# Attention totals summed behind the next product, and a 66-column spread of the maxima

## The chip, the cores and the metric

The kernel runs on one core of one Trainium2 chip. The metric is device microseconds of one execution; the runs of a kernel are given with their median.

## The reference

Two blocks run one after the other. The first is attention with hashed buckets over q, k and v of shape 4 x 8 x 768 x 64; the second is a gated MLP over the attention's output.

```python
mask = q_bucket[:, :, :, None] == k_bucket[:, :, None, :]   # 6 sign bits of q @ proj, k @ proj
scores = np.where(mask, (q @ k.T) / 8, -1e9)
attn = np.exp(scores - max(scores));  attn = attn / (attn.sum(-1) + 1e-9)
x = attn @ v                                     # heads side by side: 4 x 768 x 512
h = gelu(x @ w_in);  u, v = h[..., :512], h[..., 512:]
v_s = w_sg @ layer_norm(v) * g_ln + b_sg         # along the sequence
out = x + (u * v_s) @ w_out
```

## The kernel before, in words

**Attention.** Two heads make a pair (16 pairs), and the 768 queries of a pair are worked on in two halves of 384: 32 half pairs. `prepare` loads a pair (q, k, v), transposes q and k on TensorE (L500), splits them into a high and a low part, and computes the bucket features (L520). For each half pair:

- `largest` computes the masked scores of 128 queries against all keys (L540) and VectorE takes the maximum of each row into `mx` (L545), three times for a half pair.
- `shift` takes the minimum of the two negated maxima into column 0 and column 64 of `m` (L552, VectorE), transposes `m` by a product with the identity (L558: three matmuls, 128 weight columns each), and ScalarE copies the rows 0 and 64 of the result into the feature rows of q (L564), so that the maximum is subtracted within the next product.
- `weigh` computes the scores of 128 keys against 384 queries (L578, three products that split float32 into parts, and the features), and ScalarE takes the exponential into `p` (L582), six times. GpSimd adds the six up into `sum` (L595).
- `weighted` is the product of `p` with v (L606): 24 matmuls, in which the two heads stand in two column groups of 64 columns. `p` has a 385th column of ones, so that column 384 of the result is the sum of v over the keys.
- `finish` sums `sum` over the partitions with a product with ones (`total`, L621: eight matmuls in four column groups of 32 columns), adds 1e-9 (L624), takes the sums through DRAM to spread them (L629, L630), takes the reciprocal (L631), brings it back through DRAM to all partitions (L633, L635), and multiplies (L641). Three ScalarE instructions (L638 to L640) and a GpSimd addition (L642) put the mean of v in the place of rows that have no partner. L643 writes the half to DRAM.

A step handles two key tiles of `weigh` and, four steps ahead (`AHEAD`), one call of `largest`; a half pair has three steps.

**The MLP.** For each batch: `hidden_v` (L774), `hidden_u` (L805), `gate` (L823), `project` (L849, and the residual by transposes, L854). `weight_job` splits the float64 weights into two float32 parts on VectorE and GpSimd (L368 to L385); `gate_weights` transposes w_sg (L733).

**What sets the order.** Every piece is handed to a planner (`Plan.add`) with an engine, a cost, a priority and what it reads and writes; `Plan.order` simulates the engines and writes the order of each engine's queue out by hand. The constants at the top (`MLP`, `HID`, `AVP`, `S0P`, `PREP`, `SHIFTP`, `FINP`, `WSTEP`, `WP`) are offsets of those priorities; the lower number comes first among pieces that can start. TensorE's results go to eight PSUM banks of one tile `psb`; a score takes two banks side by side, the product, the total and the spread one each. The DMAs of the attention are issued by SyncE.

```python
plan.add(PE, 1.3 * HT, prio, product, p + [st.v], [av], form="col")          # weighted, L608
plan.add(PE, 0.375, prio, total, [sums], [tp], form="col32")                  # finish, L623
weighted(sts[n], 2 * g + AVP)                                                 # L681
finish(sts[n], hf, 2 * g + FINP)                                              # L682
```

## Time and profile before

| | |
|---|---|
| median of 3 runs | 790.71 us (790.6 to 790.88) |
| span of the profiled execution | 791.5 us |
| PE busy | 767.8 us (97%) |
| DVE, ACT, POOL busy | 536.9, 421.1, 481.0 us |
| mean granted TensorE clock | 0.993 |

The span is the time from the first to the last instruction of the one execution that was profiled; nothing of that execution's time lies outside it in the profile. It is 0.8 us over the median of the runs. PE is TensorE's matmuls, PEld its weight loads, DVE is VectorE, ACT is ScalarE, POOL is GpSimd, SP is SyncE. Matmuls overlap, so that the end of a matmul in a row lies after the start of the next; the pace is read from the starts.

### The profile page before, as it was taken

To read this page: it belongs to the slowest core of one execution; us is meant where nothing else is said; L and a number is where in the kernel's file an instruction comes from. 1 tells how busy PE (TensorE), PEld (TensorE's weight loads), DVE (VectorE), ACT (ScalarE), POOL (GpSimd) and SP (SyncE) were. 2 spreads that over 40 slices of the span, in tenths; PEclk is the share of its full clock that TensorE was granted. 3 is DMA by queue.
4 is the path that set the end of the run, shared out by engine and by line. 5 is a ranking of instruction groups with operands and counts; after the bars stand their busy time and mean duration, and the time that the engine had idled before them with its cause. 6 is when DMAs were issued, how large, how long until landed. Compare 5 with 4: busy or idle time off the path is not lost.

```text
span 791.5 us, 14719 instructions
## 1 busy us (share of the span) xinstructions
PE 767.8 (97%) x5480; PEld 613.0 (77%) x5480; DVE 536.9 (68%) x862; ACT 421.1 (53%) x742; POOL 481.0 (61%) x522
## 2 busy tenths in 40 slices
PE   4999999999999999999999999799999999999998
PEld 3777776767677676767767669798898889988996
DVE  7978888989889888666766437868932167407630
ACT  2366576666656665655655566625632266116511
POOL 1478889898878778776867774665742235404230
PEclk9899999999999999999999999999999999999999
DMA  7032443245334414321320123400115311040003
GB/s 204 23 77 69 110 116 99 70 112 124 74 97 94 104 47 91 92 70 53 82 58 25 32 54 138 144 28 28 43 64 160 100 60 41 1 150 12 1 0 133
DMA packets 99304, 60.91 MB, mean 77 GB/s; under 512 B 64288, under 2 KB 91040, under 8 KB 99232
## 3 DMA queue, kind: packets, MB, share of 16 engines
q1 hardware_dynamic: 97920, 56.94, 26.5%
q10 hardware_dynamic: 1312, 3.02, 1.2%
q8 instruction: 43, 0.70, 0.4%
q14 instruction: 29, 0.24, 0.1%
HBM read 47.16 MB, written 12.78 MB: 76 GB/s over the span
## 4 chain that ended last, share of the span: by engine, by line
PE 86%; DVE 8%; DMA 2%; ACT 1%; issue 1%; POOL 0%; DVEq 0%; ACTq 0%; POOLq 0%; SPq 0%
PE psb L578 16%; PE psb L606 16%; PE psb L823 13%; PE psb L540 10%; PE psb L849 8%; PE psb L774 6%; PE psb L805 5%; PE psb L520 5%; PE psb L500 2%; DVE mx L545 2%; PE psb L621 2%; PE psb L558 2%; PE psb L854 1%; DVE m L552 1%; DMA sq<-s 1%
## 5 line engine op out<-in xcount | busy, mean ns | idle before, releaser
L595 POOL TENSOR_TENSOR sum<-sum,p 128x384 f32<-128x384 f32 x256 | 243.6, 983 | 8.4 <-ACT p L582 8.4
L545 DVE TENSOR_REDUCE mx<-psb 128x2 f32<-128x768 f32 x192 | 174.7, 952 | 63.1 <-PE psb L540 61.8
L582 ACT ACTIVATE p<-psb 128x768 f32<-128x768 f32 x192 | 145.7, 812 | 61.6 <-PE psb L578 60.2
L606 PE MATMUL psb<-p,v 128*64 128x385 f32 x768 | 131.2, 491 | 0.0
L606 PEld LDWEIGHTS psb<-p,v 128*64 128x64 f32 x768 | 52.3, 137 | 64.0 <-issue 62.8
L595 POOL TENSOR_TENSOR sum<-p,p 128x384 f32<-128x384 f32 x64 | 64.2, 1026 | 60.9 <-ACT p L582 60.9
L540 PE MATMUL psb<-fk,fq 64*128 64x384 f32 x384 | 72.6, 372 | 2.8 <-DVE mx L545 1.7
L759 DVE SCALAR_TENSOR_TENSOR h<-h,psb 128x384 f32<-128x384 f32 (+1 forms) x56 | 32.8, 606 | 58.5 <-ACT h L758 58.5
L834 POOL TENSOR_TENSOR gs<-gt,gs 128x384 fp32r<-128x384 f32 x32 | 33.2, 1041 | 59.2 <-ACT gs L831 59.2
L578 PE MATMUL psb<-hq,hk 64*128 64x384 f32 x384 | 68.8, 352 | 0.0
L540 PE MATMUL psb<-hk,hq 64*128 64x384 f32 x384 | 65.5, 335 | 0.0
L849 PE MATMUL psb<-woh,gs 128*128 128x512 f32 x192 | 65.4, 402 | 0.0
L578 PE MATMUL psb<-fq,fk 64*128 64x384 f32 x384 | 65.1, 332 | 0.0
L578 PE MATMUL psb<-lq,hk 64*128 64x384 f32 x384 | 65.0, 332 | 0.0
L578 PE MATMUL psb<-hq,lk 64*128 64x384 f32 x384 | 64.9, 332 | 0.0
L823 PE MATMUL psb<-wgh,zh 128*128 128x384 f32 x192 | 64.3, 335 | 0.0
L823 PE MATMUL psb<-wgh,zl 128*128 128x384 f32 x192 | 64.2, 334 | 0.0
L823 PE MATMUL psb<-wgl,zh 128*128 128x384 f32 x192 | 64.2, 334 | 0.0
L540 PEld LDWEIGHTS psb<-fk,fq 64*128 64x128 f32 x384 | 36.6, 185 | 30.2 <-issue 13.0
L826 DVE TENSOR_TENSOR gt<-psb,b_bc 128x384 f32<-128x384 f32 x32 | 17.8, 556 | 58.4 <-PE psb L823 34.9
L784 POOL TENSOR_TENSOR mv<-mv,epsr 128x1 f32<-128x1 f32 x24 | 14.1, 588 | 67.8 <-DVE mv L783 67.7
L626 ACT COPY un<-psb 128x385 f32<-128x385 f32 x32 | 15.5, 483 | 68.2 <-PE psb L606 68.2
(127 smaller groups left out, 1751.8 us busy)
## 6 DMA issues: line engine op xcount, KB each, us to landing
q<-in_q_dram SPq DMA_DIRECT2D x32, 192.0 KB
k<-in_k_dram SPq DMA_DIRECT2D x32, 192.0 KB
v<-in_v_dram SPq DMA_DIRECT2D x16, 384.0 KB
rs<-r SPq DMA_DIRECT2D x64, 96.0 KB
xs<-xt SPq DMA_DIRECT2D x32, 192.0 KB
x<-xs SPq DMA_DIRECT2D x16, 384.0 KB
rx<-xs SPq DMA_DIRECT2D x96, 64.0 KB
out_dram<-ob SPq DMA_DIRECT2D x24, 256.0 KB
```

What stands on the lines that cost most here:

```text
L520: nc.tensor.matmul(fp()[:, hf, :SH], w[:, s, :], x()[:, hf * SH:(hf + 1) * SH], start=(i == 0), stop=(i == 2))
L540: nc.tensor.matmul(sc[kh]()[:, j, :SH], x[0]()[row(j), qs], x[1]()[row(j), kh * SH:(kh + 1) * SH], start=(n == 0), stop=(n == 1))
L545: plan.add(DVE, 0.95, prio, lambda kh=kh: nc.vector.tensor_reduce(mx()[:, kh, i, :], sc[kh]()[:, :, :SH], axis=AX.X, op=ALU.max, negate=Tr ...
L578: nc.tensor.matmul(sc[i]()[:, j, :SH], x()[row(j), ks], y()[row(j), cs], start=(n == 0), stop=(n == 3))
L582: plan.add(ACT, 0.81, prio, lambda i=i: nc.scalar.activation(p[i]()[:, :, :SH], sc[i]()[:, :, :SH], AF.Exp), [sc[i]], [p[i]])
L595: plan.add(POOL, 1.03, prio + 0.6, lambda i=i, j=j, first=first: nc.gpsimd.tensor_add(sums()[:, j], (first or sums)()[:, j, :SH], p[i]()[: ...
L606: nc.tensor.matmul(av()[row(j), :SH + 1], st.v()[:, j, kt, :], p[kt]()[:, j, :], start=(kt == 0), stop=(kt == NT - 1))
L774: nc.tensor.matmul(ps(), x()[:, ts_], w[:, c, FH:FF], start=(c == 0 and n == 0), stop=(c == NC - 1 and n == 2))
L805: nc.tensor.matmul(ps()[:, :SH], w[:, c, fs], x()[:, cs], start=(c == 0 and n == 0), stop=(c == NC - 1 and n == 2))
L823: nc.tensor.matmul(vp()[:, :SH], z()[:, t, fs], w()[:, t, cs], start=(t == 0 and n == 0), stop=(t == NT - 1 and n == 2))
L834: nc.gpsimd if e == POOL else nc.vector).tensor_sub(gl()[:, cs], gt(), gh()[:, cs].bitcast(F32)),
L849: nc.tensor.matmul(po(), a()[:, ts_], w()[:, f, :], start=(f == 0 and n == 0), stop=False)
```

## The change

1. `total` is no piece of its own any more. `weighted` of a half pair is given the half pair before it (`owed`) and runs the eight matmuls of its total right behind its own product, in one piece. `finish` of a half pair therefore comes one half pair later; `last` runs the one total that is left at the end. `sum` gets three buffers, `un` four.
2. The three ScalarE instructions and the GpSimd addition for rows without a partner go. The 385th column of `p` holds 1e-9 / 768 in the place of 1, and one VectorE instruction computes (un + column 384) x reciprocal.
3. `mx` has a third column that holds the constant `EMPTY`, and the minimum is a `tensor_reduce` over it in the place of a `scalar_tensor_tensor` with two operands from SBUF. The spread loads 66 columns of `m` as weights in the place of 128.
4. The priority constants change, among them those of the weight splitting (`WSTEP`, `WP`) and of the MLP's weights (`MLP`), and the planner's cost for a piece with two forms.

```diff
-MLP = {"xl": "POOL", "gm": "DVE", "gl": "POOL", "wg": 463.45, "wo": -43.61, "x": 464.83}
+MLP = {"xl": "POOL", "gm": "DVE", "gl": "POOL", "wg": 450.21, "wo": 213.95, "x": 464.55}
+NSUM = 3
-HID = 277.32
-AVP = 3.21
-S0P = 0.22
+HID = 276.04
+AVP = 2.54
+S0P = 2.0
-PREP, SHIFTP, FINP, WSTEP, WP = 4.15, -4.68, 2.34, 48.11, -68.38
+PREP, SHIFTP, FINP, WSTEP, WP = 3.93, -3.05, 8.67, 59.98, 9.42
...
-            (nc.vector if i % 2 else nc.gpsimd).memset(t[:, :, SH:SH + 1], 1.0)
+            (nc.vector if i % 2 else nc.gpsimd).memset(t[:, :, SH:SH + 1], 1e-9 / S)
...
-            plan.add(DVE, 0.16, prio, lambda: V.scalar_tensor_tensor(
-                m()[:, :, MROW::BL], mx()[:, 0], EMPTY, mx()[:, 1], op0=ALU.min, op1=ALU.min),
-                     [mx], [m], port=True)
+            W = BL + 2
+            plan.add(DVE, 0.16, prio, lambda: nc.vector.tensor_reduce(
+                m()[:, :, MROW::BL], mx(), axis=AX.X, op=ALU.min), [mx], [m])
...
-                    nc.tensor.matmul(tp()[:, i * P:(i + 1) * P], m()[:, i, :], identr, start=True, stop=True)
-            plan.add(PE, 0.33, prio, spread, [m], [tp])
+                    nc.tensor.matmul(tp()[:W, i * P:(i + 1) * P], m()[:, i, :W], identr, start=True, stop=True)
+            plan.add(PE, 0.18, prio, spread, [m], [tp])
...
+            if owed is None:
+                plan.add(PE, 1.3 * HT, prio, product, p + [v_], [av], form="col")
+            else:
+                sums, tp = owed.sum, ps_one()
+                def both():
+                    product()
+                    total(sums, tp)
+                plan.add(PE, 1.3 * HT + 0.5, prio, both, p + [v_, sums], [av, tp], form=("col", "col32"))
...
-            plan.add(PE, 0.375, prio, total, [sums], [tp], form="col32")
...
-            vm = late.ring([P, 1], F32, "vm", 3)
-            plan.add(ACT, 0.2, prio, lambda: nc.scalar.mul(vm(), un()[:, SH:SH + 1], 1.0 / S), [un], [vm])
-            plan.add(ACT, 0.62, prio, lambda: nc.scalar.activation(e(), rs(), AF.Relu, bias=less[:, 0:1], scale=2e-9), [rs], [e])
-            plan.add(ACT, 0.62, prio, lambda: nc.scalar.mul(e(), e(), vm()[:, 0:1]), [e, vm], [e])
-            plan.add(DVE, 0.56, prio, lambda: V.tensor_mul(xt(), un()[:, :SH], rs()), [un, rs], [xt], port=True)
-            plan.add(POOL, 0.98, prio, lambda: nc.gpsimd.tensor_add(xt(), xt(), e()), [xt, e], [xt])
+            plan.add(DVE, 0.56, prio, lambda: V.scalar_tensor_tensor(
+                xt(), un()[:, :SH], un()[:, SH:SH + 1], rs(), op0=ALU.add, op1=ALU.mult), [un, rs], [xt], port=True)
...
-                    weighted(sts[n], 2 * g + AVP)
-                    finish(sts[n], hf, 2 * g + FINP)
+                    owed = weighted(sts[n], hf, 2 * g + AVP, owed)
+        last(owed, 2 * g + FINP)
```

## Rows read from the trace of the kernel before

**Rows 1.** Busy time by stretch: PE, PEld, DVE, ACT, POOL, clock, DMA.
```profile
200.00:282.00 82.00, 81.64 (x712) 58.79 (x711) 73.55 (x94) 51.69 (x87) 65.76 (x70) 1.00 0.36 92
472.00:511.00 39.00, 34.86 (x185) 31.74 (x184) 30.97 (x68) 27.76 (x57) 21.15 (x22) 1.00 0.46 141
560.00:634.00 74.00, 72.16 (x375) 64.82 (x374) 28.03 (x59) 26.21 (x53) 26.21 (x29) 0.98 0.32 100
```
**Rows 2.** Chain that ended last, in order of time: start, us, what.
```profile
48.93 4.03 PE psb L606 x24
...
422.46 4.03 PE psb L606 x24
```
**Rows 3.** Timeline, PE alone, around a product and the total behind it: start, us.
```profile
200.41 4.10 PE L606 MATMUL psb<-p,v 128*64 128x385 f32 x24
204.44 0.45 PE L540 MATMUL psb<-fk,fq 64*128 64x384 f32 x2
204.72 0.34 PE L540 MATMUL psb<-hk,hq 64*128 64x384 f32 x2
204.89 0.35 PE L540 MATMUL psb<-fk,fq 64*128 64x384 f32 x2
...
206.82 0.34 PE L540 MATMUL psb<-hk,hq 64*128 64x384 f32 x2
207.11 0.44 PE L540 MATMUL psb<-fk,fq 64*128 64x384 f32 x2
207.39 0.34 PE L540 MATMUL psb<-hk,hq 64*128 64x384 f32 x2
207.66 0.53 PE L621 MATMUL psb<-sum,ones 128*32 128x192 f32 x8
208.12 0.44 PE L578 MATMUL psb<-hq,hk 64*128 64x384 f32 x2
208.41 0.33 PE L578 MATMUL psb<-hq,lk 64*128 64x384 f32 x2
```
**Rows 4.** Timeline, weight loads alone: a spread's three, then the product's in pairs.
```profile
213.09 0.41 PEld L558 LDWEIGHTS psb<-identr,m 128*128 128x128 f32 x3
213.57 0.20 PEld L606 LDWEIGHTS psb<-p,v 128*64 128x64 f32 x4
213.95 0.14 PEld L606 LDWEIGHTS psb<-p,v 128*64 128x64 f32 x2 [0.18 <-issue]
214.27 0.14 PEld L606 LDWEIGHTS psb<-p,v 128*64 128x64 f32 x2 [0.18 <-issue]
```
**Rows 5.** Weight loads grouped by line and shape: busy, mean ns, idle before.
```profile
L606 PEld LDWEIGHTS psb<-p,v 128*64 128x64 f32 x768 | 52.3, 137 | 64.0 <-issue 62.8 <-ACT e L639 0.4 <-DMA rs<-r 0.3
L558 PEld LDWEIGHTS psb<-identr,m 128*128 128x128 f32 x96 | 13.5, 193 | 8.4 <-DVE m L552 7.2 <-ACT p L582 0.7 <-issue 0.3
L621 PEld LDWEIGHTS psb<-sum,ones 128*32 128x32 f32 x256 | 5.0, 108 | 8.1 <-issue 7.5 <-POOL zl L790 0.4 <-POOL xl L707 0.3
```
**Rows 6.** Timeline around a spread that waits for its maxima.
```profile
225.08 2.10 POOL L595 TENSOR_TENSOR sum<-sum,p 128x384 f32<-128x384 f32 x2
225.23 0.89 DVE L552 SCALAR_TENSOR_TENSOR m<-mx 128x6 fp32r<-128x6 f32 x1
...
225.91 0.34 PE L520 MATMUL psb<-lq,pwh 128*128 128x384 f32 x1
...
226.18 0.55 PE L558 MATMUL psb<-identr,m 128*128 128x128 f32 x3
```
**Rows 7.** Groups by line of what goes or is replaced, and two small VectorE instructions.
```profile
L552 DVE SCALAR_TENSOR_TENSOR m<-mx 128x6 fp32r<-128x6 f32 x32 | 24.5, 766 | 1.1
L642 POOL TENSOR_TENSOR xt<-xt,e 128x384 f32<-128x384 f32 x32 | 33.8, 1055 | 13.0 <-ACT e L640 6.6 <-issue 4.9 <-DVE wx L383 0.9
L631 DVE RECIPROCAL sq<-sq 128x6 f32<-128x6 f32 x32 | 5.8, 181 | 2.5 <-DMA sq<-s 2.5
```
**Rows 8.** Timeline, POOL's last addition of the half pair of rows 3.
```profile
204.16 0.91 POOL L595 TENSOR_TENSOR sum<-sum,p 128x384 f32<-128x384 f32 x1
```
**Rows 9.** Timeline of the start: VectorE's first weight splitting, TensorE's first transposes.
```profile
7.88 0.29 DVE L374 TENSOR_SCALAR wy<-wx 128x256 int32<-128x256 int32 x1
...
8.25 1.51 PE L500 MATMUL psb<-ident,q 128*128 128x128 f32 x6 [2.65 <-DVE wy L374]
```
**Rows 10.** Timeline: the two copies of the spread's rows into the features.
```profile
213.68 0.47 ACT L564 CAST fq<-psb 1x384 fp32r<-1x384 f32 x1 [0.16 <-PE psb L558]
...
215.34 0.47 ACT L564 CAST fq<-psb 1x384 fp32r<-1x384 f32 x1
```

More of the change, by code (lines that the diff above doesn't have):

```diff
@@ L171, in order @@
             if e == "PE":
-                work = g["c"] + (self.TURN_PE[g["form"]] if g["form"] != form else 0.0)
-                form = g["form"]
+                one, two_ = g["form"] if isinstance(g["form"], tuple) else (g["form"],) * 2
+                work = g["c"] + (self.TURN_PE[one] if one != form else 0.0)
+                form = two_
                 at_, cost = start, 0.0
@@ L290 @@
     nc.vector.memset(ones, 1.0)
-    less = const.tile([P, 1], F32, name="less")
-    nc.vector.memset(less, -1.0)
     tiny = const.tile([P, 1], F32, name="tiny")
@@ L328 @@
     nc.vector.memset(fv[:, 3, :, MROW:MROW + 1], 1.0)
+    mxs = [const.tile([P, HT, 2, 3], F32, name=f"mx{i}") for i in range(3)]
+    for t in mxs:
+        nc.vector.memset(t[:, :, :, 2:3], EMPTY)
     msts = [const.tile([P, HT, P], F32R, name=f"m{i}") for i in range(2)]
@@ L569, in weigh @@
             if k0 == 0:
-                st.sum, st.p = held.ring([P, 2, SH], F32, "sum", 2), []
+                st.sum, st.p = held.ring([P, 2, SH], F32, "sum", NSUM), []
             sums, sc, p = st.sum, [ps_two() for _ in kts], [p_tile() for _ in kts]
@@ L596, in weigh, with weighted @@
                             sums()[:, j], (first or sums)()[:, j, :SH], p[i]()[:, j, :SH]), [p[i]] + ([first] if first else []), [(sums, j)])
-        def weighted(st, prio):
-            st.av, p = ps_one(), st.p
-            av = st.av
+        def weighted(st, hf, prio, owed):
+            av, p, v_ = ps_one(), st.p, st.v
+            half = Pair()
+            half.n, half.b, half.hp, half.hf, half.av, half.sum = st.n, st.b, st.hp, hf, av, st.sum
             def product():
@@ L605, in product @@
                     for j in range(2):
-                        nc.tensor.matmul(av()[row(j), :SH + 1], st.v()[:, j, kt, :], p[kt]()[:, j, :], start=(kt == 0), stop=(kt == NT - 1))
-            plan.add(PE, 1.3 * HT, prio, product, p + [st.v], [av], form="col")
-        def finish(st, hf, prio):
-            av, sums, tp = st.av, st.sum, ps_one()
-            sm, e = late.ring([P, QH2], F32, "sm", 3), late.ring([P, SH], F32, "e", 3)
+                        nc.tensor.matmul(av()[row(j), :SH + 1], v_()[:, j, kt, :], p[kt]()[:, j, :], start=(kt == 0), stop=(kt == NT - 1))
@@ new lines, in weighted @@
+            if owed is None:
[6 more added lines that the diff above has]
+                plan.add(PE, 1.3 * HT + 0.5, prio, both, p + [v_, sums], [av, tp], form=("col", "col32"))
+            half.un = un = late.ring([P, SH + 1], F32, "un", 4)
+            plan.add(ACT, 0.48, prio - 1, lambda: nc.scalar.copy(un(), av()[:, :SH + 1]), [av], [un])
@@ new lines, in weighted, with total, last @@
+            if owed is not None:
+                finish(owed, tp, prio)
+            return half
+        def total(sums, tp):
+            for j in range(2):
+                for a in range(2):
+                    r = 64 * j + 32 * a
+                    nc.tensor.matmul(tp()[r:r + 32, :QH2], ones, sums()[:, j, a * QH2:(a + 1) * QH2], start=True, stop=True)
+        def last(half, prio):
+            sums, tp = half.sum, ps_one()
+            plan.add(PE, 0.375, prio, lambda: total(sums, tp), [sums], [tp], form="col32")
+            finish(half, tp, prio)
@@ L614, in finish @@
+        def finish(st, tp, prio):
+            hf, un = st.hf, st.un
+            sm = late.ring([P, QH2], F32, "sm", 3)
             sq, rs, xt = late.ring([P, W6], F32, "sq", 3), late.ring([P, SH], F32, "rs", 3), late.ring([P, SH], F32, "xt", 2)
             V = nc.vector
-            def total():
-                for j in range(2):
-                    for a in range(2):
-                        r = 64 * j + 32 * a
-                        nc.tensor.matmul(tp()[r:r + 32, :QH2], ones, sums()[:, j, a * QH2:(a + 1) * QH2], start=True, stop=True)
```

8 lines of the change are left out of this document (3 added, 5 removed).

## The prediction

> **What bounds the kernel.** I read the busy time by stretches first. In the middle of the attention TensorE is busy for 81.64 of 82 us at full clock, and VectorE, the next, for 73.55 [rows 1]. So in this stage the time is what TensorE's queue takes; another engine matters only where its lateness opens a hole there. The chain that ended last says the same by its products with v: one every (422.46 - 48.93) / 27 = 13.83 us for a half pair [rows 2]. Busy time alone hides what matters here, since matmuls overlap. So I went on to TensorE's timeline and read the pace from the starts: a pair of 384-column matmuls in two row groups starts every 0.17 us (204.72 to 204.89), and where the next one starts later, time is lost [rows 3]. In the MLP, holes are left in two stretches only: 39.0 - 34.86 = 4.1 us at 472 to 511 and 1.8 us at 560 to 634 [rows 1].
>
> **The total as a piece of its own.** Without it the pair that starts at 208.41 would have started two paces of 0.175 behind the one at 207.39, at 207.74. The total costs 208.41 - 207.74 = 0.67 us [rows 3]. I split it. The last pair ahead of it ends its pace at 207.565 and the total starts at 207.66: 0.10 for going in. From its start to the next piece's are 0.46. Behind it the second pair comes after 0.29 instead of 0.175: 0.11 [rows 3]. Of the 0.46 a part is again the way out. The product shows how much: its weight loads come in pairs every 0.32 us [rows 4], twelve pairs make 3.87, but the next piece starts 204.44 - 200.41 = 4.03 after it, so 0.16 is the way out, and the 0.11 follows there too (204.44 to 204.72 is 0.28) [rows 3]. So the total is 0.10 in, 0.30 work, 0.16 and 0.11 out.
>
> Behind the product the way out is paid once for both. What stays is the work, 0.30, and what it costs to go from columns of 64 to columns of 32, which the trace before never does. Bounds: nothing, if the eight matmuls follow like any others; or 0.16, as much as a way out. I take 0.10, the price of going in from row groups, the nearest row. The saving is 0.67 - 0.40 = 0.27, bounds 0.21 and 0.37, in 31 half pairs (the last total stays alone): **8.4 us, from 6.5 to 11.5**.
>
> The Trainium skill (TensorEngine Tiling (Array Packing), Key Properties) says that changing the tiling mode, as opposed to the tile, drains TensorE. By it the step from 64 to 32 columns is not free, and the sum stays at 8.4 or goes towards 6.5; without a drain it would be 11.5. The ways in and out above agree with it for row against column; no row has one column form behind another.
>
> The piece now waits for `sum` of the half pair before. That was complete at 204.16 + 0.91 = 205.07 [rows 8], 8.5 us ahead of the next product, which begins to load at 213.57 [rows 4], so this wait costs nothing; if GpSimd fell back by those 8.5 us, it would hold the whole queue of TensorE. The six DMAs of each `finish` (sums out, in, reciprocal out, two back, result out) come some 6 us later in SyncE's queue; behind them stand the loads of the next pair, which `prepare` asks for 8 units of priority (four steps) ahead of its transposes, and the MLP reads the first batch, done after 24 of 192 steps, only from `HID` on, step 138. I cost it at nothing; a late load would show as TensorE waiting at L500.
>
> **The spread.** The three loads of 128 columns take 0.41 from the first start to the last end, and one is 0.19, so they start every 0.11 us [rows 4]. The matmuls between stream 128 columns each, a third of what takes 0.175, so the loads set the pace. A load of 32 columns lasts 108 ns, of 64 columns 137, of 128 columns 193 [rows 5]: about 0.9 ns for each column. 62 columns fewer are 54 ns for a load if nothing else takes over the pace. The matmul does: 0.175 / 3 is 0.06. So the pace goes from 0.11 to about 0.065, and three of them in 32 half pairs save 3 x 0.045 x 32 = **4.3 us**. Bounds: 0, if something else holds the pace, and 3 x 0.054 x 32 = 5.2.
>
> **The minimum.** L552 takes 766 ns in the mean for six elements to a partition, beside 181 for a reciprocal of the same size [rows 7]; in [rows 6] it lasts 0.89 while GpSimd's addition with two operands runs. It ends at 226.12, and the spread starts at 226.18, 0.27 behind the last feature matmul instead of 0.175: a wait of 0.095. The replacement reads one operand and, if it is like the reciprocal, lasts 0.2 and ends 0.6 us earlier: the wait goes. The feature matmuls come ahead of the spread in 14 of the 32 half pairs, so 14 x 0.095 = **1.3 us**; bounds 0 (the reduction is held up like the old one) and 3.
>
> **What goes on the other engines.** GpSimd's 33.8 us [rows 7] and ScalarE's three instructions are off TensorE's path and give nothing; their cover is the product itself. They make the exponentials and sums a little earlier. VectorE's multiplication stays one instruction, with a third operand; nothing. The memsets are the same in number.
>
> **The priorities.** At the start the first weight splitting stands ahead of the first pair on VectorE and in the load queue, and TensorE's first transposes wait 2.65 us, by the profile until L374 [rows 9]. With `WP` at 9.42 these jobs come behind the first pair. I take **1.0 us**, bounds 0 and 3; below nothing is excluded, since the jobs are only moved to where VectorE is free. The MLP's offsets move the splitting of w_out behind other work and w_sg ahead of the loads of x; the most they can win is the 4.1 + 1.8 us of holes [rows 1], the most they can lose I put at as much again. I take nothing.
>
> **The sum.** 8.4 + 4.3 + 1.3 + 1.0 = 15.0 us from the span of 791.5: 776.5. The span stood 0.8 over the median of the runs; I predict the median, 790.7 - 15.0 = **775.7 us**. With all lower bounds (6.5, and nothing else) it is 784.2; with the upper ones 790.7 - 22.7 = 768.0, and less still if the stall of the next part goes.
>
> **Rivals.**
>
> *The gain turns into waits for PSUM.* In the step after the product TensorE already waits: 206.82 to 207.11 is 0.29 instead of 0.175, and another 0.11 follows [rows 3]. The score there wants two of eight banks, which an exponential or a reduction has to leave first. The total's 0.67 stood right behind this and gave VectorE and ScalarE time to catch up. Without it the next scores may wait in its place. VectorE's 73.55 of 82 us allow 13.83 x 0.897 = 12.4 us for a half pair, and the forecast needs 13.83 - 0.27 - 0.13 - 0.04 = 13.39; so there is room in the mean, and only bunched work can stall. If it takes back 10 of the 15.0 us: 786. The opposite case: the stall before the total, 0.22 in nearly every half pair, goes with the new order; up to 31 x 0.22 = 6.8 us more, to 769, or below 768 with other upper bounds.
>
> *A narrow load is no faster.* If 128 columns are loaded on a faster path than fewer, so that 66 columns need their whole 139 ns (137 plus two columns of 0.9), one after the other, three loads go from 0.11 to 0.14 each: a loss of 3 x 0.03 x 32 = 2.9 us in the place of 4.3 gained, and 775.7 + 7.2 = 782.9. Against it: the three widths lie on one line [rows 5]. The Trainium skill (TensorE: Matmul & The Clock Gate, Weight-path perf modes) has such a rule: fast weight load is on for 128 weights of a type other than FP32, and 66 columns would switch it off. These weights are float32 by their size in a reduced mode, and the rows show no quick load of 128 columns; so I give it little.
>
> *The other side: the maxima come too late.* `S0P` puts `largest` about one step later. If the third maximum then comes right ahead of the product, the spread goes behind the product, and the scores after it wait for ScalarE's copies of its rows. From the start of the spread at 213.12 to the end of the second copy are 215.34 + 0.47 - 213.12 = 2.69 us [rows 10]. Less the spread (0.45) and one step's maxima (0.8) TensorE waits 1.44 us in 31 half pairs: 45 us, and 775.7 + 45 is 821. Today the product of 4.03 us covers it. It turns slower than before from a wait of 15.0 / 31 = 0.48 us in a half pair. What speaks for it is only the moved offset; `SHIFTP` and `AVP` move too.
>
> **How the numbers follow.** The forecast, with each term within its bounds: 0.66 (768 to 782). More than that, below 768: 0.07. Narrow load no faster: 0.07. Waits take back most of it, 782 to 789: 0.10. Waits take it all back: 0.04. Maxima too late, or another hole of half a microsecond in each half pair: 0.06. A difference of 0.2% (1.6 us) is about what can be told from no change. So faster 0.90, same 0.04, slower 0.06. The range goes from 767 to 786: it holds the forecast, the narrow load and half of the waits, about 8 in 10.
>
> **What would show it.** In the profile after: L621 in 31 of 32 places right behind L606, with no row-group piece between, and some 0.40 us from its first matmul's regular time to the regular way out; half pairs of about 13.4 us; the spread's three loads some 0.065 apart and about 139 ns long; its minimum at 0.2 us. Wrong would be: starts of L540 or L578 that are late by tenths of a microsecond in each half pair with ScalarE or VectorE named (waits for PSUM), L578 waiting for the copies of L564 (late maxima), or a longer MLP with new holes at w_sg or w_out.

## The result, and the profile after

The changed kernel takes 768.17 us (median of 4 runs, 766.59 to 768.48) beside 790.8 us for the kernel before in the same session. The ratio on record is 0.9698, with a 95% interval from 0.9679 to 0.9716; the two medians by themselves make 0.9714. Two repeats gave 0.9682 [0.9657, 0.9706] and 0.9702 [0.9687, 0.9716]. The three medians of the changed kernel (768.17, 767.21, 768.34) have a mean of 767.9, and the three differences to the kernel before a mean of (22.6 + 24.8 + 23.6) / 3 = 23.7 us. Forecast were 15.0. So the direction was right, and the gain is half as large again.

The page's first part, after:

```profile
span 764.8 us, 14521 instructions
PE 745.1 (97%) x5480; PEld 607.6 (79%) x5480; DVE 531.3 (69%) x864; ACT 389.2 (51%) x646; POOL 454.4 (59%) x490
```

The profiled execution took 766.59 us, 1.8 us more than its span. All executions for which both are on record, those of the kernel before too (792.13 and 790.3), lasted 1.7 to 1.9 us longer than their span. By that the profiled execution of the kernel before lasted some 793.3 us (an estimate) and not 791.5, its span: it was one of the slower ones, and differences of these two spans come out 3 us larger (791.5 - 764.8 = 26.7) than those of the times (23.7). PE's busy time fell by 767.8 - 745.1 = 22.7 us: what went is time in which TensorE counted as busy. Busy time by stretch, with the columns of [rows 1]:

```profile
200.00:282.00 82.00, 82.00 (x751) 62.45 (x751) 71.11 (x97) 49.58 (x76) 65.37 (x69) 1.00 0.35 89
560.00:634.00 74.00, 74.00 (x372) 63.87 (x372) 33.10 (x68) 31.62 (x60) 23.87 (x28) 1.00 0.28 90
```

TensorE is still busy all the time in the attention, but gets through 751 matmuls in the 82 us in which it did 712 [rows 1]. The busy share of an engine whose work overlaps says nothing of its pace. The chain that ended last (start, us, what) shows the pace by its products with v:

```profile
32.67 4.03 PE psb L609 x24
...
203.01 4.03 PE psb L609 x24
...
398.99 4.03 PE psb L609 x24
```

Fifteen half pairs take 398.99 - 203.01 = 195.98 us, 13.07 each. The same fifteen of before stand in its chain between the product at 213.64 and the one at 422.46 [rows 2]: 13.92 each. By place: the first product starts at 32.67 us, and 37.40 before, so 4.7 us are won ahead of it; the next 28 half pairs take 366.3 instead of 422.46 - 37.40 = 385.1, 18.7 less; and the rest (three half pairs and the MLP) 764.8 - 398.99 = 365.8 instead of 369.0, 3.2 less, of which three half pairs at 0.85 make 2.6. The MLP itself hardly moved.

TensorE's timeline around a product and the total behind it, beside [rows 3]:

```profile
202.94 4.10 PE L609 MATMUL psb<-p,v 128*64 128x385 f32 x24
206.97 0.53 PE L631 MATMUL psb<-sum,ones 128*32 128x192 f32 x8
207.43 0.44 PE L543 MATMUL psb<-fk,fq 64*128 64x384 f32 x2
207.71 0.34 PE L543 MATMUL psb<-hk,hq 64*128 64x384 f32 x2
207.89 0.34 PE L580 MATMUL psb<-hq,hk 64*128 64x384 f32 x2
```

From product to total are 4.03, from total to the next pair 0.46, and the second pair follows after 0.28. In [rows 3] the next piece also starts 4.03 behind the product and its second pair 0.28 later: so the total now costs the 0.46 alone, where it cost 0.67. And the scores for the maxima (L543) and the weights (L580) now stand one of each in turn; in [rows 3] two maxima's scores stand together, with the stall at 206.82 to 207.11 between them.

The spread between feature matmuls, beside [rows 6]; the first line is the piece behind the spread in the trace of before, the others are of the changed kernel:

```profile
226.56 0.40 PE L520 MATMUL psb<-hk,pwh 128*128 128x384 f32 x1
...
214.85 0.34 PE L523 MATMUL psb<-lq,pwh 128*128 128x384 f32 x1
215.03 0.34 PE L560 MATMUL psb<-identr,m 128*66 128x128 f32 x3
215.21 0.39 PE L523 MATMUL psb<-hk,pwh 128*128 128x384 f32 x1
```

It starts 0.18 behind the feature matmul, and the next one 0.18 behind it, where [rows 6] had 0.27, and 226.18 to 226.56, 0.38. The groups of its weight loads and of its minimum, beside [rows 5, 7], and the three loads ahead of a product, beside the first line of [rows 4]:

```profile
L560 PEld LDWEIGHTS psb<-identr,m 128*66 128x66 f32 x96 | 10.0, 137 | 2.4 <-DVE m L555 0.9 <-issue 0.4 <-ACT p L584 0.2
L555 DVE TENSOR_REDUCE m<-mx 128x6 fp32r<-128x18 f32 x32 | 5.5, 173 | 1.1
...
202.56 0.31 PEld L560 LDWEIGHTS psb<-identr,m 128*66 128x66 f32 x3
```

A load takes 137 ns instead of 193, the three together 0.31 us instead of 0.41, the minimum 173 ns instead of 766. The idle time in the loads' row is what to look at: of their idle time 0.9 us ended with the minimum (L555), and in [rows 5] 7.2 us ended with L552.

### The profile page after: what moved, and what is told of

Its sections match the earlier page's. It is cut to its first block, busy times and chain, and to the rows that moved or that the text cites. A ratio compares the mean times of both kernels' runs of the same rounds, so it can differ in the third digit from the quotient of the medians.

```text
span 764.8 us, 14521 instructions
## 1 busy us (share of the span) xinstructions
PE 745.1 (97%) x5480; PEld 607.6 (79%) x5480; DVE 531.3 (69%) x864; ACT 389.2 (51%) x646; POOL 454.4 (59%) x490
## 4 chain that ended last, share of the span: by engine, by line
PE 84%; DVE 7%; DMA 4%; issue 2%; POOL 1%; ACT 1%; SPq 1%; DVEq 0%; ACTq 0%; POOLq 0%
PE psb L580 16%; PE psb L609 15%; PE psb L839 12%; PE psb L865 9%; PE psb L543 8%; PE psb L821 6%; PE psb L790 6%; PE psb L523 4%; PE psb L503 3%; PE psb L631 2%; PE psb L870 1%; DVE mx L548 1%; POOL sum L597 1%; DMA ow<-in_moe_w_out_dram 1%; DMA q<-in_q_dram 1%
## 5 line engine op out<-in xcount | busy, mean ns | idle before, releaser
L597 POOL TENSOR_TENSOR sum<-sum,p 128x384 f32<-128x384 f32 x256 | 249.0, 1010 | 0.0
L548 DVE TENSOR_REDUCE mx<-psb 128x2 f32<-128x768 f32 x192 | 181.0, 956 | 45.1 <-PE psb L543 37.2
L584 ACT ACTIVATE p<-psb 128x768 f32<-128x768 f32 x192 | 155.4, 815 | 62.3 <-PE psb L580 56.2
L543 PE MATMUL psb<-fk,fq 64*128 64x384 f32 x384 | 68.4, 353 | 2.1 <-DVE fk L526 1.3
L580 PE MATMUL psb<-hq,hk 64*128 64x384 f32 x384 | 65.6, 338 | 2.0 <-DVE mx L548 1.1
L580 PE MATMUL psb<-fq,fk 64*128 64x384 f32 x384 | 64.5, 332 | 0.0
L543 PE MATMUL psb<-hk,hq 64*128 64x384 f32 x384 | 64.4, 332 | 0.0
L580 PE MATMUL psb<-hq,lk 64*128 64x384 f32 x384 | 64.4, 332 | 0.0
L580 PE MATMUL psb<-lq,hk 64*128 64x384 f32 x384 | 64.3, 331 | 0.0
L806 POOL TENSOR_TENSOR zl<-y,zh 128x512 fp32r<-128x512 f32 x24 | 32.3, 1348 | 25.4 <-ACT zh L805 25.3
```

Source lines behind the costliest of these rows:

```text
L543: nc.tensor.matmul(sc[kh]()[:, j, :SH], x[0]()[row(j), qs], x[1]()[row(j), kh * SH:(kh + 1) * SH], start=(n == 0), stop=(n == 1))
L548: plan.add(DVE, 0.95, prio, lambda kh=kh: nc.vector.tensor_reduce(mx()[:, i, :, kh], sc[kh]()[:, :, :SH], axis=AX.X, op=ALU.max, negate=Tr ...
L580: nc.tensor.matmul(sc[i]()[:, j, :SH], x()[row(j), ks], y()[row(j), cs], start=(n == 0), stop=(n == 3))
L584: plan.add(ACT, 0.81, prio, lambda i=i: nc.scalar.activation(p[i]()[:, :, :SH], sc[i]()[:, :, :SH], AF.Exp), [sc[i]], [p[i]])
L597: plan.add(POOL, 1.03, prio + 0.6, lambda i=i, j=j, first=first: nc.gpsimd.tensor_add(sums()[:, j], (first or sums)()[:, j, :SH], p[i]()[: ...
```

## The experiments

Line numbers of a kernel shift by a few with its edit. Ratios are to the kernel before on the same chip, differences to the 767.9 us of the changed kernel. The kernel before had medians of 790.8 to 792.65 us in the sessions, and most of the ratios' intervals reach 1 to 2 us to either side, so a single term is not known better than that.

**The changed kernel again, twice**

> The changed kernel once more, beside the next three on the same chip: the same time as before this within half a per cent, 766 to 771 us.

> The changed kernel once more, as the measure for the next two on the same chip: 766 to 769 us.

Told above; the medians agree within 1.2 us, so smaller differences than that are not read below.

**The total as a piece of its own**

```diff
...
+            plan.add(PE, 1.3 * HT, prio, product, p + [v_], [av], form="col")
...
-                    owed = weighted(sts[n], hf, 2 * g + AVP, owed)
+                    last(weighted(sts[n], hf, 2 * g + AVP, None), 2 * g + 2.34)
```

> The changed kernel with the total as a piece of its own again; everything else, the constants too, as changed. The order written out keeps a score of the maxima and a score of weigh in turn. If a total of its own costs only its second way in and out (0.67 against 0.46 us, read from the profile after), 31 half pairs cost 6.5 us: 774.7. If it was the total that also caused the 0.22 us of stall ahead of it, the stall comes back: 31 x 0.43 = 13.3, 781.5.

778.86 us, 0.9826 [0.981, 0.9843], 11.0 slower than the changed kernel. The order of scores stays one of each in turn. Its timeline:

```profile
258.40 0.34 PE L580 MATMUL psb<-fq,fk 64*128 64x384 f32 x2
258.67 0.53 PE L620 MATMUL psb<-sum,ones 128*32 128x192 f32 x8
259.13 0.45 PE L543 MATMUL psb<-fk,fq 64*128 64x384 f32 x2
259.42 0.34 PE L543 MATMUL psb<-hk,hq 64*128 64x384 f32 x2
...
262.21 0.34 PE L580 MATMUL psb<-fq,fk 64*128 64x384 f32 x2
262.82 0.44 PE L543 MATMUL psb<-fk,fq 64*128 64x384 f32 x2 [0.26 <-DVE mx L548]
```

The total costs 0.10 in (0.27 for 0.175), 0.46, and 0.11 out again: 0.21 more than behind the product, 6.5 us in 31 half pairs. The last fifteen half pairs (211.57 to 412.75 in the chain) take 13.41 instead of 13.07, so 0.345 more. The rest is a new wait for VectorE's maxima, 0.61 instead of 0.175 at 262.82, in 4 of the 15: 4 x 0.44 / 15 = 0.12, and 0.21 + 0.12 = 0.33. The undoing moves VectorE's and ScalarE's work too; the merge by itself is the 6.5.

**The total with 64 columns, so that its form is the product's**

```diff
-    ones = const.tile([P, 32], F32, name="ones")
+    ones = const.tile([P, 64], F32, name="ones")
...
-                for a in range(2):
-                    r = 64 * j + 32 * a
-                    nc.tensor.matmul(tp()[r:r + 32, :QH2], ones, sums()[:, j, a * QH2:(a + 1) * QH2], start=True, stop=True)
+                nc.tensor.matmul(tp()[row(j), :SH], ones, sums()[:, j, :], start=True, stop=True)
...
```

> The changed kernel, in the same order, with the total in the product's own form: ones of 64 columns, two matmuls of 384 columns in the place of four of 192, so that no form changes behind the product; the 385-column pair of the product lasts 0.32 us and two such pairs are streamed. If the 0.16 us between product and total is the price of the change from 64 to 32 columns, the gap goes and the work rises from 0.30 to 0.64: 31 x 0.18 = 5.6 us more than the changed kernel. If the gap has another cause (the wait for the sum, the new PSUM bank), it stays: 31 x 0.34 = 10.5 us more.

772.7 us, 0.9754 [0.9728, 0.9779], 4.8 slower:

```profile
245.48 4.10 PE L609 MATMUL psb<-p,v 128*64 128x385 f32 x24
249.41 0.81 PE L629 MATMUL psb<-sum,ones 128*64 128x384 f32 x4
250.16 0.45 PE L543 MATMUL psb<-fk,fq 64*128 64x384 f32 x2
```

The total starts 3.93 behind the product instead of 4.03. So going from 64 to 32 columns costs 0.10, and 3.93 - 3.87 = 0.06 lies there without it. The four matmuls of 384 columns take 0.75 where the eight of 192 took 0.46. This shows in one row what the prediction could only bound: the way from one column form to the other costs as much as into the total from row groups.

**128 weight columns in the spread**

```diff
-            W = BL + 2
+            W = P
```

> The changed kernel with 128 weight columns in the spread, planned at the same cost, so the order of every engine is the same. If the loads set the pace, three loads a spread cost 0.05 us each more: 32 x 0.15 = 4.8 us, 773.0. If something else holds the pace or the product hides it: 768.2.

771.11 us, 0.9727 [0.9706, 0.9748], 3.2 slower, with the same order on each engine.

```profile
217.04 0.45 PE L560 MATMUL psb<-identr,m 128*128 128x128 f32 x3
217.33 0.39 PE L523 MATMUL psb<-hk,pwh 128*128 128x384 f32 x1
```

The next piece comes 0.29 behind the spread instead of 0.18, 0.11 in each of 32 half pairs: 3.5 us, and 3.2 measured. "A narrow load is no faster" falls.

**The minimum with two operands again**

```diff
-            plan.add(DVE, 0.16, prio, lambda: nc.vector.tensor_reduce(
-                m()[:, :, MROW::BL], mx(), axis=AX.X, op=ALU.min), [mx], [m])
+            plan.add(DVE, 0.16, prio, lambda: nc.vector.scalar_tensor_tensor(
+                m()[:, :, MROW::BL], mx()[:, :, :, 0], EMPTY, mx()[:, :, :, 1], op0=ALU.min, op1=ALU.min), [mx], [m])
```

> The changed kernel with the two-operand minimum of before, in the same order. If the 0.77 us that it took before held up the spread, 14 to 32 half pairs lose 0.1 us: 1.3 to 3.2 us, 769.5 to 771.4, and the instruction lasts 0.8 us again. If the new order leaves room between the last maximum and the spread: 768.2 although it lasts as long.

771.71 us, 0.9735 [0.972, 0.9749], 3.8 slower, same order. The instruction takes 506 ns in the mean here, and 173 in the changed kernel. Its late half pairs go at 13.08, as in the changed kernel: the loss is early. In this order the minimum is worth less than in that of before, as the next one shows.

**The spread and its minimum alone, in the order of before**

```diff
-                    mx()[:, kh, i, :], sc[kh]()[:, :, :SH], axis=AX.X, op=ALU.max, negate=True), [sc[kh]], [(mx, (kh, i))])
+                    mx()[:, i, :, kh], sc[kh]()[:, :, :SH], axis=AX.X, op=ALU.max, negate=True), [sc[kh]], [(mx, (kh, i))])
...
+            plan.add(DVE, 0.16, prio, lambda: V.tensor_reduce(m()[:, :, MROW::BL], mx(), axis=AX.X, op=ALU.min),
...
-                    nc.tensor.matmul(tp()[:, i * P:(i + 1) * P], m()[:, i, :], identr, start=True, stop=True)
+                    nc.tensor.matmul(tp()[:BL + 2, i * P:(i + 1) * P], m()[:, i, :BL + 2], identr, start=True, stop=True)
```

> The kernel before, in its own order, with the spread of 66 columns and the one-operand minimum alone. The prediction has 4.3 + 1.3 = 5.6 us: 786.4. From the profile after, a spread behind the feature products is 0.30 us shorter and one ahead of the product 0.13 us: 16 x 0.43 = 6.9, 785. If the saved time turns into waits for PSUM: 792.

781.82 us, 0.9871 [0.9856, 0.9885]: 791.63 - 781.82 = 9.8 us, where the prediction's two terms make 5.6. Where they come from stands in the trace of before, in a place that the prediction didn't read, a spread between the transposes of q and k:

```profile
239.13 0.88 PE L500 MATMUL psb<-ident,q 128*128 128x128 f32 x6
240.37 0.55 PE L558 MATMUL psb<-identr,m 128*128 128x128 f32 x3 [0.36 <-DVE m L552]
```

VectorE's minimum runs from 239.44 to 240.32 there, and the spread starts 1.24 behind the transposes; where nothing waits it is 0.57 (185.17 to 185.74). Six half pairs of before have this, at 1.21 to 1.24: 6 x 0.66 = 4.0 us. Between features the wait costs more than its own 0.10: with 128 columns and no wait the next matmul came after 0.29 (above), behind the late spread after 0.38, so another 0.09. There are 13 such places (116.22 has no wait, and the first spread stands where the clock is low): 13 x 0.19 = 2.5. With the loads' 3.2 to 3.5 that is 9.7 to 10.0. In this kernel no spread waits behind the transposes (0.57 to 0.63 after the start of their six matmuls), and 15 half pairs of its chain go from 210.33 to 412.91: 13.505 each. The stall ahead of the total is still there:

```profile
203.65 0.34 PE L543 MATMUL psb<-hk,hq 64*128 64x384 f32 x2
203.94 0.44 PE L543 MATMUL psb<-fk,fq 64*128 64x384 f32 x2
204.22 0.33 PE L543 MATMUL psb<-hk,hq 64*128 64x384 f32 x2
```

**The offset of the maxima as before**

```diff
-S0P = 2.0
+S0P = 0.22
```

> The changed kernel with S0P at 0.22: the total stays behind the product, but the order written out has two scores of the maxima in a row, then two of weigh, as before. If the stall of 0.22 us in each half pair came from that grouping (two scores in a row find their PSUM banks not yet left), it comes back: 31 x 0.22 = 6.8 us, 775.0. If it came from the total, the time stays at 768.2.

776.17 us, 0.9791 [0.9775, 0.9808], 8.3 slower. With this one number the maxima's scores stand in pairs again, and the stall of 0.11 and 0.11 comes back, twice in each half pair:

```profile
200.69 0.33 PE L543 MATMUL psb<-hk,hq 64*128 64x384 f32 x2
200.97 0.45 PE L543 MATMUL psb<-fk,fq 64*128 64x384 f32 x2
201.25 0.34 PE L543 MATMUL psb<-hk,hq 64*128 64x384 f32 x2
```

The last fifteen half pairs take 13.47 each (207.00 to 409.08), 0.40 more. The total still stands behind the product. So the order of the scores, not the merge, takes the stall away.

**Constants on the old code**

```diff
-S0P = 0.22
+S0P = 2.0
```

> The kernel before with S0P at 2.0 alone: the spread comes behind the product in some half pairs and two scores of weigh stand in a row twice. If late maxima stall TensorE, it is slower than before, by up to 1.4 us in 16 half pairs (22 us): 792 to 814. If other work fills in, it is as before or faster by the stall of 0.22 us: 785 to 791.

832.73 us, 1.051 [1.0493, 1.0528]. And with all of the change's constants but `FINP` in the code of before:

```diff
-MLP = {"xl": "POOL", "gm": "DVE", "gl": "POOL", "wg": 463.45, "wo": -43.61, "x": 464.83}
+MLP = {"xl": "POOL", "gm": "DVE", "gl": "POOL", "wg": 450.21, "wo": 213.95, "x": 464.55}
...
-HID = 277.32
-AVP = 3.21
-S0P = 0.22
+HID = 276.04
+AVP = 2.54
+S0P = 2.0
...
-PREP, SHIFTP, FINP, WSTEP, WP = 4.15, -4.68, 2.34, 48.11, -68.38
+PREP, SHIFTP, FINP, WSTEP, WP = 3.93, -3.05, 2.34, 59.98, 9.42
```

> The kernel before with all the priority constants of the changed one, FINP apart; its code as it was. The order written out now takes a score of the maxima and one of weigh in turn, and puts the spread behind the product in every second half pair. If the constants alone carry the gain that is not in the total, the spread or the minimum, it is 5.3 (start) + 1.8 (MLP) + 31 x 0.22 = 14 us faster than before: 778. If a spread behind the product makes TensorE wait for the copies of its rows, as one rival of the prediction has it (1.4 us each in 16 half pairs), that takes it back: 790 to 800.

885.35 us, 1.1175 [1.1154, 1.1196]. The order is now the one that the rival "the maxima come too late" feared, on the code that the constants don't belong to: the spread stands behind the product (first of the two, timeline; so in 15 of 32 half pairs):

```profile
221.26 2.11 PE L606 MATMUL psb<-p,v 128*64 128x385 f32 x12
223.30 0.55 PE L558 MATMUL psb<-identr,m 128*128 128x128 f32 x3
```

but the wait is another than that rival's. TensorE's loads hardly wait for the copies of the spread's rows (L564: 0.6 us in all in the first, 0.4 in the second). They wait for exponentials and maxima, as in the rival "the gain turns into waits for PSUM" (waits of the second, with the total, the times and the longest):

```profile
PEld psb L578 <- ACT p L582: 41.8, 70, 1.2
PEld psb L540 <- DVE mx L545: 27.7, 55, 4.2
```

So these constants lose time on the code of before: code and offsets fit only together. Which of the constants turns 832.73 into 885.35 was not tested.

**The weight splitting as early as before**

```diff
-PREP, SHIFTP, FINP, WSTEP, WP = 3.93, -3.05, 8.67, 59.98, 9.42
+PREP, SHIFTP, FINP, WSTEP, WP = 3.93, -3.05, 8.67, 48.11, -68.38
```

> The changed kernel with WSTEP and WP of before (48.11 and -68.38), so that the first weight splitting stands ahead of the first pair again. If this is what made the first product come 4.7 us earlier (32.67 against 37.40 us), the first product comes at 36 to 38 us again and the time is 4 to 5 us more than the changed kernel's. If the earlier start came from elsewhere (the order of the maxima, the shorter minimum, the granted clock), the first product stays near 33 us and the time is the same within 1 us.

772.54 us, 0.9741 [0.9712, 0.9769], 4.6 slower, and the first product starts at 37.41, as before (37.40). VectorE shows the first part of the delay, in the trace of this experiment and then in the changed kernel's:

```profile
18.20 0.68 DVE L373 TENSOR_SCALAR wy<-w 128x256 int32<-128x256 int32 x1
18.91 0.42 DVE L374 SCALAR_TENSOR_TENSOR wx<-w,wy 128x256 int32<-128x256 int32 x1
19.25 5.27 DVE L548 TENSOR_REDUCE mx<-psb 128x2 f32<-128x768 f32 x6
```

```profile
17.10 5.27 DVE L548 TENSOR_REDUCE mx<-psb 128x2 f32<-128x768 f32 x6
```

The first maxima come 2.15 us later, behind the splitting. The second part comes after them, where VectorE splits weights between the maxima and TensorE waits for it. TensorE in this experiment, and then the score in the changed kernel that stands in the place of the first line:

```profile
26.94 0.44 PE L543 MATMUL psb<-fk,fq 64*128 64x384 f32 x2
...
29.20 0.44 PE L580 MATMUL psb<-hq,hk 64*128 64x384 f32 x2 [0.60 <-DVE fk L526]
...
31.97 0.44 PE L543 MATMUL psb<-fk,fq 64*128 64x384 f32 x2 [0.59 <-DVE mx L548]
...
33.68 0.45 PE L543 MATMUL psb<-fk,fq 64*128 64x384 f32 x2 [0.40 <-DVE mx L548]
```

```profile
24.39 0.45 PE L543 MATMUL psb<-fk,fq 64*128 64x384 f32 x2
```

At that score the delay is 26.94 - 24.39 = 2.55 us; up to the first product it grows to 37.41 - 32.67 = 4.7, in three places where TensorE starts 0.57 to 0.77 us later than its pace. Between the first maxima and that score the clock falls as well. Windows of this experiment, then of the changed kernel:

```profile
20.00:25.00 5.00, 4.75 (x18) 3.47 (x19) 4.96 (x8) 0.00 (x0) 0.00 (x0) 0.50 0.11 23
25.00:30.00 5.00, 4.39 (x34) 3.67 (x32) 4.90 (x9) 2.17 (x4) 0.00 (x0) 0.88 0.17 54
```

```profile
20.00:25.00 5.00, 4.30 (x27) 3.21 (x28) 4.97 (x9) 1.75 (x3) 0.00 (x0) 1.00 0.35 79
25.00:30.00 5.00, 5.00 (x58) 4.54 (x56) 4.90 (x6) 3.19 (x4) 2.10 (x3) 1.00 0.01 3
```

With the splitting early the granted clock is 0.50 of full speed at 20 to 25 us, the lower level, 1.2 GHz; in the changed kernel it is 1.00. Ahead of the fall TensorE had less to do: at 15 to 20 us it was busy for 2.33 us here (2.61 in the kernel before, whose clock fell to 0.76), and for 3.35 in the changed kernel. The fall costs little: from the first maxima to the score behind the features are 26.94 - 19.25 = 7.69 us with it and 24.39 - 17.10 = 7.29 without it (27.81 - 19.37 = 8.44 in the kernel before, whose clock was still low, 0.56, at 25 to 30 us). And one of the four executions of this experiment had a mean clock of 1.000 and still took 770.9 us, where the changed kernel's at 0.999 and 1.000 took 766.42 to 767.83. So the 4.6 us are in the main VectorE's lateness.

**The MLP's offsets as before**

```diff
-MLP = {"xl": "POOL", "gm": "DVE", "gl": "POOL", "wg": 450.21, "wo": 213.95, "x": 464.55}
+MLP = {"xl": "POOL", "gm": "DVE", "gl": "POOL", "wg": 463.45, "wo": -43.61, "x": 464.83}
```

> The changed kernel with the three MLP offsets of before; the attention's order up to the MLP is the same. From the 29th product to the end the changed kernel is 3.2 us shorter, of which three half pairs explain 1.3 to 2.5. If the offsets gave the rest, the time rises by 1 to 2 us; if not, it is the same within 1 us.

769.03 us, 0.9703 [0.968, 0.9726], 1.1 over the changed kernel and within its repeats: no effect that this can tell.

**The chain for rows without a partner**, in three ways. First, in the order of before, planned but not issued:

```diff
-            plan.add(ACT, 0.62, prio, lambda: nc.scalar.mul(e(), e(), vm()[:, 0:1]), [e, vm], [e])
...
+            plan.add(ACT, 0.62, prio, lambda: None, [e, vm], [e])
...
+            plan.add(POOL, 0.98, prio, lambda: None, [xt, e], [xt])
```

> The kernel before without the three ScalarE instructions and the GpSimd addition (the changed kernel's column of 1e-9 / 768 and its one VectorE instruction instead), planned as before at their costs, so that the order of all other instructions is that of before. If they are off the path there, as the prediction has it: 792, the same. If they hold up the maxima there too: 2 to 15 us less.

792.46 us, 1.001 [1.0001, 1.0019] in 11 runs: 0.8 us and not a gain. Then the chain put back into the changed kernel, once with the planner free to order it anew, and once with that order but without its instructions:

```diff
...
+            plan.add(ACT, 0.62, prio, lambda: nc.scalar.activation(e(), rs(), AF.Relu, bias=less[:, 0:1], scale=2e-9), [rs], [e])
+            plan.add(ACT, 0.62, prio, lambda: nc.scalar.mul(e(), e(), vm()[:, 0:1]), [e, vm], [e])
...
+            plan.add(POOL, 0.98, prio, lambda: nc.gpsimd.tensor_add(xt(), xt(), e()), [xt, e], [xt])
```

> The changed kernel with the three ScalarE instructions and the GpSimd addition of before in the place of the one VectorE instruction, and ones in the 385th column. If they are off TensorE's path, as the prediction has it, the time is that of the changed kernel within 1 us: 768. If GpSimd's 34 us or ScalarE's 46 us are on the path in the part of the attention where weights are split as well, it is 2 to 6 us more.

> The kernel of e10 (the changed kernel, the mean's chain planned freely) with the chain planned but not issued, and the one VectorE instruction in its place; the order of all that is left is e10's. If the order that the planner wrote for the chain was what gave 808 us, it stays near 800 to 808. If the chain's own instructions did, it falls to 768 to 775.

807.94 us, 1.0201 [1.0184, 1.0218], and 805.29 us, 1.0168 [1.0154, 1.0182]. Slower than the kernel before both times, and only 2.7 us apart: almost all of it is the order that the planner writes out once it counts four more pieces. (Both have one buffer for `e`, where the kernel before has three; what the order would be with three was not tested.) At last the instructions in place of one VectorE piece, so that the order of the changed kernel stays:

```diff
...
+                V.tensor_mul(xt(), un()[:, :SH], rs())
+                nc.scalar.activation(rs(), rs(), AF.Relu, bias=less[:, 0:1], scale=2e-9)
+                nc.scalar.mul(rs(), rs(), vm[:, 0:1])
+                nc.gpsimd.tensor_add(xt(), xt(), rs())
...
```

> The changed kernel with the three ScalarE instructions and the GpSimd addition of before again (they work in place on the reciprocal's tile, behind VectorE's multiplication, to need no more memory), and ones in the 385th column. They are issued where the one VectorE instruction stood, so that the order of all other instructions on every engine is that of the changed kernel; with the planner free, the same instructions gave 808 us. If it was the order written out that cost 40 us, and the instructions are off TensorE's path, the time is the changed kernel's within 1.5 us. If GpSimd's 34 and ScalarE's 46 us are themselves in the way (they delay exponentials and, by the port that VectorE and GpSimd share, the maxima), it is 3 to 40 us more.

784.26 us, 0.9905 [0.9888, 0.9921], 16.4 slower. The waits of VectorE and of the loads in this kernel:

```profile
DVE lq L513 <- ACT hq L510: 25.9, 14, 3.1
...
PEld psb L546 <- DVE mx L551: 13.2, 21, 2.1
```

ScalarE's two instructions of 0.62 us write over an operand of VectorE's multiplication, so they come behind it (7.0 us of waits in all), and they stand ahead of ScalarE's copy of q (L510). VectorE's next work waits for that copy for 25.9 us in all (9.5 in the changed kernel), the maxima come late, and TensorE waits for those. So removing the chain is worth nothing in the order of before and 16 us in this one, put in at this place; how much of the 16 comes from working in place, which the chain of before did not, was not tested.

**Two totals behind every second product**

```diff
-            if owed is None:
+            if len(owed) < 2:
...
-                    total(sums, tp)
+                    for sums, tp in pairs:
+                        total(sums, tp)
```

> The changed kernel with the totals of two half pairs behind every second product, so that the way in and out of the 32-column form is paid 15 times in the place of 31. If the total behind the product costs 0.16 us of change and 0.30 us of work, as read from the profile, it saves 15 x 0.16 = 2.4 us: 765.5. If the 0.46 us are work, it saves nothing: 768.

771.78 us, 0.9747 [0.9732, 0.9761]. And with the last half pair's product taking what is owed, so that one total is left at the end:

```diff
...
+            now = len(owed) == 2 or (st.n == NPAIR - 1 and hf == 1)
...
```

> The totals of two half pairs behind every second product, but with one total behind the last product as in the changed kernel, so that the end of the attention is the same. Two totals behind every second product made the attention up to the 29th product 2.9 us shorter, which is 14 times 0.2, but lost 6 us in the MLP. If the loss came from the two totals at the end, this version is 2 to 3 us faster than the changed kernel: 765. If it came from elsewhere in the MLP's order, 771 again.

767.81 us, 0.9698 [0.9682, 0.9713], the same as the changed kernel. From the first product to the 29th the first of these takes 396.86 - 33.18 = 363.7 us, where the second profile of the changed kernel has 399.06 - 32.49 = 366.6: 2.9 less. The rows give 1.8 of it: two totals in a row take 0.79 us to the next piece (from 400.89, 4.03 behind the product at 396.86), and two single ones 2 x 0.46 = 0.92, so 0.13 is saved 14 times. By this a total's work is 0.33 and its way out 0.13. The other 1.1 us are not explained. What is won is given back later: from that product to the end are 765.4 - 395.94 = 369.5 us in the second of them, 366.9 in the changed kernel (766.0 - 399.06). Why is not shown.

## Why the prediction was right, and where it was wrong

The direction and most mechanisms were right, but the sum of 15.0 us was 8.7 short of the 23.7 measured. The step that failed is the term for the minimum, priced at 1.3 us and worth 6.6; the start (1.0 against 4.6) is the second. Both lie outside their own bounds of 3. That the time still fell inside the range of 767 to 786 is partly luck, since the total and the loads came out below their values.

| term | forecast, us | measured, us | from |
|---|---|---|---|
| total behind the product | 8.4 (6.5 to 11.5) | 6.5 | 0.46 instead of 0.67, 31 times |
| loads of the spread | 4.3 (0 to 5.2) | 3.2 | 128 columns again |
| minimum | 1.3 (0 to 3) | 6.6 | spread alone (9.8) less the loads |
| priorities, start | 1.0 (0 to 3) | 4.6 | early splitting again |
| stall ahead of the total | 0 (a rival, up to 6.8) | 2.8 | what is left of 23.7 |
| chain, MLP's offsets | 0 | 0 in the order of before; 1.1, within the repeats | chain not issued; old offsets |

The terms are measured in different orders of the queues (the old minimum costs 3.8 us in the changed kernel's order and 6.6 in that of before), so the stall's 2.8 carries their differences. It carries the offsets HID, AVP, PREP and SHIFTP too, which were not put back by themselves.

**What bounds the kernel** was read rightly: TensorE's queue in the attention, paced by the starts.

**The total.** The parts were near: two totals in a row make 0.33 for the work and 0.13 for the way out, where the prediction had 0.30 and 0.16. Between product and total lie 0.16 and not the 0.10 taken. The 64-column run lays 0.10 of them to the change of form, as forecast; the other 0.06 are there without a change, and the sum had put them at nothing. So the term came out at its lower bound. The Trainium skill (TensorEngine Tiling (Array Packing), Key Properties) has a drain on a change of the tiling mode; the 3.93 against 4.03 agree with it for one column form behind another.

**The loads.** 137 ns is what the two other widths gave, but ahead of the product the three start (0.31 - 0.137) / 2 = 0.087 apart and not 0.065. From the first start to the last end 0.10 us are saved for each spread (0.41 to 0.31), where the prediction had 0.135. The run with 128 columns shows the whole term. The Trainium skill's rule of a fast weight load (TensorE: Matmul & The Clock Gate, Weight-path perf modes), on for 128 weights of a type other than FP32, would have made 128 columns the quicker if it held for these; 190 ns against 137 show no sign of it here.

**The minimum is the step that failed**, a term mis-sized by a factor of five. The mechanism was named: the instruction beside GpSimd's addition ends late, and the spread waits. But it was priced from one place (0.095 at 226.18) times the 14 half pairs with features ahead. The 0.09 that a late spread costs behind itself was left out, and the six spreads behind transposes, where the wait cost 0.66 each, were not looked at. [rows 5] pointed there: the loads' idle time that ended with L552 is 7.2 us, and it is 0.9 after. It was a hint and not a price: the matmuls of the spread show 2.4 us of idle time behind L552 in the kernel before.

**The start is the second**: the delay was taken from TensorE's first transposes [rows 9], which come before VectorE's delay has reached anything. The place to read was the first product, 37.40, and what VectorE does ahead of it: the splitting puts the first maxima 2.15 us back and makes TensorE wait for VectorE three times more.

**The chain's removal** was costed at nothing, and in the order of before that is so. That it makes room for the new order (16 us if it is put back there) was not foreseen: an engine off the path that delays what the path needs next, not its own busy time, sets that price.

**The rivals.** The narrow load fell. The gain did not turn into waits for PSUM; the opposite case came, in part. In the last fifteen half pairs the steps close: 0.415 for the spread and minimum (13.92 - 13.505), 0.21 for the merge and 0.22 for the stall make 0.845, and 13.92 - 13.07 = 0.85 was measured. Ahead of those a part is lost again to waits that the changed kernel has while VectorE still splits weights:

```profile
143.90 0.34 PE L543 MATMUL psb<-hk,hq 64*128 64x384 f32 x2
144.81 0.44 PE L580 MATMUL psb<-hq,hk 64*128 64x384 f32 x2 [0.57 <-ACT p L584]
```

There are six such places at L543 and L580 between the first product and 205 us, 1.9 us in all over the pace. The first thirteen half pairs take (203.01 - 32.67) / 13 = 13.10 each, (213.64 - 37.40) / 13 = 13.56 before: 0.46 less, not 0.85. Of the 0.39 x 13 = 5.1 us between, the six waits take 1.9 and their ways out 6 x 0.11 = 0.7; and five of before's six late spreads lie in the last fifteen half pairs (5 x 0.66 / 15 = 0.22 each) and one in the first thirteen (0.05 each), which makes 2.2. The last 0.3 stay open.

The order that the rival of the late maxima feared came on the old code, at 832.73 and 885.35 us, with waits for PSUM in the place of waits for the copies; in the changed kernel it did not come. On the new code the offset S0P draws the scores of the maxima apart; on the old code it pushes the spread behind the product as well. What exactly in the new code lets it do the one without the other (the total gone from between, or ScalarE's chain) is not settled by single edits; putting the planned chain back (805.29) turns the gain into a loss, which speaks for the chain.

## What to carry to other kernels

Check the price of a wait, taken from one place, against the row that sums the wait over the kernel (here the idle time of a group and what ended it): where the two are five times apart, as here, look for places of another kind. The row alone is no price either. In the changed kernel the loads of the total show 10.2 us of idle time that ended with GpSimd's sum, and its matmuls none. When the queues' order is written out by a planner, a piece taken off an idle engine may be worth nothing in the old order and much in the new one, so judge code and offsets together. And work on an engine that looks free at the start can delay the first stage: read the start by the first product, not by the first matmul.

## What the runs showed of the hardware

- Going from a product in 64-column tiles to one in 32-column tiles costs TensorE 0.10 us (4.03 against 3.93 us from the product's start to the next piece).
- A weight load of 66 columns takes 137 ns, as one of 64 columns does [rows 5], and three in a row start 0.087 us apart; with 128 columns it is 190 ns and 0.11.
- A VectorE instruction on six elements of a partition took 766 ns in the mean with two operands from SBUF, 506 in another order, and 173 as a reduction of one operand of 18 elements: its size doesn't set its time. In [rows 6] GpSimd's addition with two operands runs beside it.
- The granted clock at 20 to 25 us was 0.50 with the early offsets of the weight splitting and 1.00 with the late ones, nothing else being changed. It was 0.66 with the late ones where the total is a piece of its own, and the first product came at 33.28 all the same (32.67 in the changed kernel): the early splitting is not needed for the fall, and here the fall is little of what delays the start.
